# Four nested conditionals for leftover tiles instead of 36, and a plan of 23 places instead of 55

## The chip, the core and the metric

The kernel runs on one core of a Trainium2 chip. The metric is the device time of one execution in microseconds (us); the time given is the median of several executions.

## What is computed

Two blocks follow each other. The first is a gated linear recurrence over 4 batches, 8 heads, 768 steps and head dimension 48; its output, laid out as 3072 rows of 384, is the input of a mixture of 8 experts, of which each row takes two, chosen by noisy logits.

```python
for t in range(S):
    state = alpha[:, :, t, :, None] * state + np.einsum('bhd,bhe->bhde', k[:, :, t], v[:, :, t])
    y[:, :, t] = np.einsum('bhd,bhde->bhe', q[:, :, t], state)
...
noisy_logits = x @ w_gate + np.log1p(np.exp(x @ w_noise)) * noise
top2 = np.argpartition(-noisy_logits, 2, axis=1)[:, :2]
top2_l = top2_l - top2_l.max(-1, keepdims=True)
top2_w = np.exp(top2_l)
top2_w /= top2_w.sum(-1, keepdims=True) + 1e-09
for e in range(E):
    for k in range(2):
        mask = top2[:, k] == e
        h = np.maximum(x[mask] @ w1[e], 0.0)
        out[mask] += top2_w[mask, k, None] * (h @ w2[e])
```

All is float32. With N = 3072 rows and two experts for each there are 6144 row-expert entries, 768 for each expert on average. w1 of an expert is 384 x 1024, w2 is 1024 x 384.

## The kernel before

**Recurrence.** The 3072 steps are worked in NT = 24 chunks of C = 128. The order of the work is written out by hand in the block at the end of the kernel function; the loop over chunks issues loads, transposes, scans, scores, state and output of neighbouring chunks interleaved. Rows of the result go to x_rows in HBM. The routing of a unit of six chunks (`routing`) is a generator; each call of `route` or `route_on` runs its next piece, so that small vector operations are strewn among the others. Entries (row, gate, other expert, rank) are scattered by indirect transfers into `table`, which has a region of 3072 rows for each expert.

**Pairs.** 24 fixed steps follow, `pair_steps`, each for 256 entries of one expert: three for every expert, first one each, then two each. A step has a list of times on a scale where a pair takes T = 20; `work` sorts the steps of all pairs, of the half tiles and of `beside()` by these times, and `until` issues them in that order. A pair gathers its rows by index, multiplies by w1 and w2 on TensorE (PE) with sums formed on VectorE (DVE), scales by the gate on ScalarE (ACT), adds the row of an earlier expert (`get_prev`, `combine`) and scatters the result to the output (`put_pair`). The indirect transfers are issued by GpSimd (POOL), weights by SyncE (SP).

**Leftovers.** 24 pairs hold 768 entries of each expert. What an expert has above that goes to half tiles of 64 entries, of which there are places for NHALF = 3 (`half_tiles`), worked between pairs, and then to whole tiles of 128. Whole tiles stand behind a conditional at the end of the kernel: `more_i` is the number of such tiles plus `again`, a count of rows for which the fast form of the recurrence is not valid. If it is above zero, `last_tiles` works tile after tile, each one nested in the conditional of the tile before, NFULL = 36 deep; then, if `again_i` (the count of rows alone) is above zero, `again_by_levels` does everything anew in a general way, with 24 chunks by levels and 55 tiles.

```python
any_more = nc.values_load(more_i[0:1, 0:1], min_val=0, max_val=NTILE + 3 * C,
...
with tc.If(any_more > 0):
    ...
    redo = nc.values_load(again_i[0:1, 0:1], min_val=0, max_val=3 * C,
    ...
    with tc.If(redo > 0):
```

**Plan.** Where the tiles of variable place begin is computed on DVE in `plan_rest`, once all counts are known (`counted`, `tiles_of`, L774 and L776). `plan` has NTILE = 55 places: 3 half tiles, 16 for the second and third pairs, 36 whole tiles. For each place `given` holds, per expert, how many entries earlier places have taken (55 x 9 values per partition); `first_rows` makes from it the expert (column 0 of plan, L803) and the first row of the table (column 1, L810). The larger operations are L853 and L855 (`gone`), L858 (`given`), L787, L789 and L862 (the share of whole tiles), L794 and L796 in `begun`, and L801, L805, L807, L809 in `first_rows`. `base_of` is a constant of the same shape, set on POOL in `place_slots` (L129 to L142). The pieces are issued by `route_on(3)` in the eighth and the tenth pair. Readers of the plan are `of_plan` (L891), a register load on SP or POOL, ahead of the loads of table rows and weights for half tiles and for the later pairs, and `find_rows` and `choose_rows`, which read `given`.

`out_of_range` (L452 to L457) makes `again` at the sixth pair, and before the change its integer copy `again_i` (L456).

Sequencer instructions of the conditional carry the line L1408, the register load of its count L1406, and what stands at the end of the program L1443.

Of the kernel before, what the change touches and what calls it, by code (L numbers as in the profile page):

```python
# [9 lines left out]
F32 = mybir.dt.float32  # L10
# [3 lines left out]
ALU = mybir.AluOpType  # L14
# [4 lines left out]
def kernel(  # L19
# [32 lines left out]
    nc = tc.nc  # L52
    B, H, S, D = q.shape
    N, DM = out.shape
    E, _, F = moe_w1.shape
    C = 128
# [10 lines left out]
    HC = C // 2  # L67
# [3 lines left out]
    EV = E + 1  # L71
    NTILE = (2 * N) // C + E - 1
# [4 lines left out]
    R2 = 2 * C  # L77
# [2 lines left out]
    AFTER_GROUP = (3, 5, 7)  # L80
    FIRST_PAIR = NHALF
    FIRST_FULL = NHALF + 2 * E
    NFULL = NTILE - FIRST_FULL
    assert R2 * NPAIR == 2 * N and NFULL * C >= 2 * (N - 3 * R2)

    def pool(name, bufs, on=ctx, **kw):
        return on.enter_context(tc.tile_pool(name=name, bufs=bufs, **kw))
# [33 lines left out]
                   allow_small_or_imprecise_dtypes=True)  # L121

    half_no = const.tile([C, NTILE], F32, name="half_no")
    base_of = const.tile([C, NTILE, EV], F32, name="base_of")
    of_slot = const.tile([C, NTILE], F32, name="of_slot")

    def place_slots():
        pairs = base_of[:, FIRST_PAIR:FIRST_FULL].rearrange("p (g b) e -> p g b e", b=2)
        nc.gpsimd.memset(base_of, float(3 * R2))  # L129
        nc.gpsimd.affine_select(out=pairs, in_=pairs, pattern=[[1, E], [0, 2], [1, EV]], compare_op=ALU.is_gt,  # L130
                                fill=float(R2), base=1 - E, channel_multiplier=0)
        nc.gpsimd.affine_select(out=pairs[:, :, 1], in_=pairs[:, :, 1], pattern=[[1, E], [1, EV]],
                                compare_op=ALU.not_equal, fill=float(2 * R2), base=1 - E, channel_multiplier=0)
        nc.gpsimd.iota(of_slot[:, FIRST_PAIR:FIRST_FULL], pattern=[[-1, E], [0, 2]], base=E - 1, channel_multiplier=0,
                       allow_small_or_imprecise_dtypes=True)
        groups = (0,) + AFTER_GROUP + (E,)
        for j in range(NHALF):
            nc.gpsimd.memset(base_of[:, j, 0:E - AFTER_GROUP[j]], float(R2))
            nc.gpsimd.memset(half_no[:, j:j + 1], float(j))
        for j in range(NHALF + 1):  # L140
            nc.gpsimd.memset(half_no[:, FIRST_PAIR + 2 * groups[j]:FIRST_PAIR + 2 * groups[j + 1]], float(j))
        nc.gpsimd.memset(half_no[:, FIRST_FULL:NTILE], float(NHALF))  # L142


    x_rows = dram.tile([N, DM], F32, name="x_rows")
# [133 lines left out]
    def fast_gla(on):  # L279
# [169 lines left out]
        def out_of_range(part):  # L449

            if part:
                out_of = chunks["out_of"]  # L452
                count = few(on, [C, 3], "count", True)
                nc.tensor.matmul(count, ones, out_of[:, 2:5], start=True, stop=True)
                nc.vector.tensor_reduce(out=again, in_=count[0:1, :], axis=mybir.AxisListType.X, op=ALU.add)
                nc.vector.tensor_copy(out=again_i, in_=again)  # L456
                return  # L457
            out_of = chunks["out_of"] = one.tile([C, 5], F32, name="out_of")
            nc.vector.tensor_copy(out=out_of[:, 4:5], in_=short)
            nc.vector.tensor_reduce(out=out_of[:, 0:1], in_=P_end.rearrange("p n j -> p (n j)"),  # L460
                                    axis=mybir.AxisListType.X, op=ALU.min)
            nc.vector.tensor_reduce(out=out_of[:, 1:2], in_=above, axis=mybir.AxisListType.X, op=ALU.max)
            nc.vector.tensor_scalar(out=out_of[:, 2:3], in0=out_of[:, 0:1], scalar1=2 * RANGE, scalar2=None,
                                    op0=ALU.is_lt)
            nc.vector.tensor_scalar(out=out_of[:, 3:4], in0=out_of[:, 1:2], scalar1=0.0, scalar2=None, op0=ALU.is_gt)
# [330 lines left out]
        nc.vector.reduce_sum(out=of, in_=behind, axis=mybir.AxisListType.X)  # L796

    def first_rows(rp, of):
        shape = [C, NTILE, EV]
        behind = rp.tile(shape, F32, name="behind")  # L800
        nc.vector.tensor_tensor(behind, expert_idv[:, None, :].to_broadcast(shape), of[:, :, None].to_broadcast(shape),  # L801
                                op=ALU.is_equal)
        nc.vector.tensor_scalar(out=plan[:, :, 0], in0=of, scalar1=float(E - 1), scalar2=None, op0=ALU.min)  # L803
        at = rp.tile(shape, F32, name="at_row")
        nc.vector.tensor_tensor(at, given, region[:, None, :].to_broadcast(shape), op=ALU.add)  # L805
        yield
        nc.vector.tensor_mul(at, at, behind)  # L807
        first = rp.tile([C, NTILE], F32, name="first")
        nc.vector.reduce_sum(out=first, in_=at, axis=mybir.AxisListType.X)  # L809
        nc.vector.tensor_scalar(out=plan[:, :, 1], in0=first, scalar1=float(TROWS - C), scalar2=None, op0=ALU.min)  # L810

    def plan_all(on):
        rp = on["one"]
# [9 lines left out]
            pass  # L823

    def plan_rest(on):

        rp = on["one"]
        total = counted(on)
# [15 lines left out]
        start, ends = running(rp, ready)  # L844
        nc.vector.tensor_copy(out=tiles_i, in_=ends[0:1, E - 1:E])
        nc.vector.tensor_tensor(more_i, ends[0:1, E - 1:E], again, op=ALU.add)
        yield
        begun(rp, of_slot[:, 0:NHALF], tile_no[:, 0:NHALF], which)
        begun(rp, of_slot[:, FIRST_FULL:NTILE], tile_no[:, 0:NFULL], ends)
        yield  # L850
        shape = [C, NTILE, EV]
        gone = rp.tile(shape, F32, name="at_row")
        nc.vector.tensor_tensor(gone, half_no[:, :, None].to_broadcast(shape), which[:, None, :].to_broadcast(shape),  # L853
                                op=ALU.is_ge)
        nc.vector.tensor_tensor(gone, gone, half[:, None, :].to_broadcast(shape), op=ALU.mult)  # L855
        yield
        fulls = given[:, FIRST_FULL:NTILE]
        nc.vector.scalar_tensor_tensor(given, gone, float(HC), base_of, op0=ALU.mult, op1=ALU.add)  # L858
        yield
        at = rp.tile(shape, F32, name="behind")[:, 0:NFULL]  # L860
        of_expert(at, NFULL, start, ready)
        nc.vector.scalar_tensor_tensor(fulls, at, float(C), fulls, op0=ALU.mult, op1=ALU.add)  # L862
        yield
        yield from first_rows(rp, of_slot)


    WHY = "computed from the counts, in range by construction"
# [94 lines left out]


    def last_tiles(i, whole_tile):
        if i == NFULL:
            return
        number = nc.values_load(tiles_i[0:1, 0:1], min_val=0, max_val=NTILE,
                                skip_runtime_bounds_check_because="a count of tiles")
        with tc.If(number > i):
            whole_tile(FIRST_FULL + i)  # L970
            last_tiles(i + 1, whole_tile)
# [436 lines left out]
    with tc.If(any_more > 0):  # L1408
        with ExitStack() as es:
            order.update(puts=[], gets=[])  # L1410
            last_tiles(0, whole_tiles(pools(es, "l_")))
        redo = nc.values_load(again_i[0:1, 0:1], min_val=0, max_val=3 * C,
                              skip_runtime_bounds_check_because="a count of at most 3 C rows")
        with tc.If(redo > 0):
            taken.clear()
            order.update(puts=[], gets=[])
            again_by_levels()
# [30 lines left out]
```

## Time and profile before

| what | value |
|---|---|
| median of 3 runs | 691.13 us (690.56 to 694.62) |
| the profiled execution | 710.9 us, its span 709.2 us |
| PE busy | 675.1 us (95% of the span) |
| DVE busy | 455.0 us (64%) |
| POOL busy | 300.4 us (42%) |
| ACT busy | 260.3 us (37%) |
| mean granted TensorE clock | 0.983 |
| last matmul ends | 692.0 us |
| last scatter to the output is issued | 693.4 us |

The span runs from the first to the last instruction of the profiled execution. Busy times are those of the engines; register loads, branches, semaphore waits and the issuing of transfers are sequencer instructions and not counted as busy. In lists, L853 is line 853 of the kernel, "xcount" the number of instructions, the number after the bar the busy time in us and the mean ns of one. In a timeline the columns are start and length in us, engine, line, operation, output <- inputs, shapes, and in brackets how long the engine had been idle and what released it. A line of a wait table reads: who waited, for whom, us in total, times, longest.

### The profile page before, as it was taken

What the parts mean: (1) busy time and instruction counts of PE and PEld (TensorE: products, weight loads), DVE (VectorE), ACT (ScalarE), POOL (GpSimd) and SP (SyncE); (2) the same over time, 40 slices, a digit from 0 to 9 for tenths busy, and PEclk for the clock granted to TensorE, in tenths of its full rate; (3) what the DMA queues carried; (4) which work ended last, traced back from release to release, by engine and by line L of the source; (5) the groups of instructions that cost most, each with busy time, mean ns of one, the idle gap of its engine ahead of it and who ended that gap; (6) DMA issues with size and microseconds to landing.
All of it is one profiled execution on the core that took longest, in us unless ns stands there. A gap on an engine that the chain in (4) does not pass through costs nothing.

```text
span 709.2 us, 15155 instructions
## 1 busy us (share of the span) xinstructions
PE 675.1 (95%) x5777; PEld 628.9 (89%) x5777; DVE 455.0 (64%) x1058; ACT 260.3 (37%) x561; POOL 300.4 (42%) x390
## 2 busy tenths in 40 slices
PE   7999999999999997999999999999999999999990
PEld 5888877878999997989999999988999889999890
DVE  8777867856778774877466667464565646645440
ACT  4456545444443323222333332333332233323330
POOL 5442483764234573586322335412453224533121
PEclk9999999999999998999999999999999999999996
DMA  9777576567866754575413457137351574521110
GB/s 177 169 154 156 129 135 136 127 129 212 285 201 221 224 150 129 198 198 189 141 37 123 136 193 261 54 130 271 117 199 60 174 251 135 157 60 38 32 45 24
DMA packets 145861, 105.64 MB, mean 149 GB/s; under 512 B 110931, under 2 KB 133151, under 8 KB 145780
## 3 DMA queue, kind: packets, MB, share of 16 engines
q1 hardware_dynamic: 134132, 80.41, 40.8%
q0 software_dynamic: 11504, 23.76, 10.8%
q8 instruction: 48, 0.79, 0.5%
q10 hardware_dynamic: 144, 0.41, 0.2%
q14 instruction: 33, 0.27, 0.1%
HBM read 95.19 MB, written 14.96 MB: 155 GB/s over the span
## 4 chain that ended last, share of the span: by engine, by line
PE 53%; issue 6%; POOL 1%; another core or an unknown queue 1%; ACT 1%; DMA 1%; DVE 0%; POOLq 0%; ACTq 0%; DVEq 0%
PE sc L1127 22%; PE o_ps L1134 13%; PE h_ps L1134 10%; PE h_ps L1127 4%; PE x_ps L1065 2%; PE half_ps L1297 1%; PE h_half_ps L1283 1%; DMA out_dram<-prev,where 1%; POOL out_dram L879 0%; POOL prev L871 0%; POOL x_in L886 0%; ACT L651 0%; ACT m L1205 0%; ACT m L1203 0%
## 5 line engine op out<-in xcount | busy, mean ns | idle before, releaser
L886 POOL DMA_INDIRECT x_in<-x_rows,where x48 | 52.6, 1095 | 138.0 <-PE h_ps L1134 87.8
L871 POOL DMA_INDIRECT prev<-out_dram,where x48 | 54.1, 1127 | 67.4 <-issue 29.6
L1127 PE MATMUL sc<-xs,ws 128*128 128x128 f32 x576 | 74.5, 279 | 2.2 <-ACT m L1205 1.9
L879 POOL DMA_INDIRECT out_dram<-prev,where x48 | 51.7, 1076 | 58.7 <-DVE prev L1155 43.3
L1127 PE MATMUL sc<-xt,w 128*128 128x128 f32 x576 | 73.9, 279 | 0.0
L1127 PEld LDWEIGHTS sc<-xs,ws 128*128 128x128 f32 x576 | 69.1, 194 | 3.1 <-ACT m L1205 2.5
L1134 PE MATMUL o_ps<-wt,hx 128*128 128x192 f32 x384 | 70.6, 327 | 0.2 <-issue 0.2
L1127 PEld LDWEIGHTS sc<-xt,w 128*128 128x128 f32 x576 | 70.8, 196 | 0.0
L1138 ACT ACTIVATE h<-h 128x512 f32<-128x512 f32 x72 | 45.4, 631 | 64.1 <-DVE h L1074 60.9
L1074 DVE TENSOR_TENSOR h<-sc,m 128x512 f32<-128x512 f32 x48 | 33.1, 692 | 50.0 <-PE sc L1127 45.1
L1134 PEld LDWEIGHTS o_ps<-wt,hx 128*128 128x128 f32 x384 | 63.5, 190 | 0.9 <-issue 0.5
L161 POOL DMA_INDIRECT table<-entry,place_u x48 | 53.0, 1105 | 15.9 <-issue 14.6
L1127 PE MATMUL sc<-xs,w 128*128 128x128 f32 x384 | 49.3, 282 | 1.2 <-DVE h L1074 1.2
L1127 PEld LDWEIGHTS sc<-xs,w 128*128 128x128 f32 x384 | 44.9, 192 | 4.8 <-DVE h L1074 3.8
L369 POOL TENSOR_TENSOR k_P<-k_P,over 128x512 f32<-128x512 f32 (+1 forms) x25 | 28.8, 1153 | 47.8 <-DVE over L353 36.5
L1127 PE MATMUL h_ps<-xt,w 128*128 128x128 f32 x384 | 47.1, 276 | 0.0
L326 PE MATMUL tp<-ident,ins 128*128 128x128 f32 x288 | 42.9, 285 | 4.0 <-issue 2.9
L1127 PEld LDWEIGHTS h_ps<-xt,w 128*128 128x128 f32 x384 | 44.8, 192 | 0.2
L1143 ACT ACTIVATE o<-o_ps,tab 128x192 f32<-128x192 f32 x23 | 9.6, 419 | 96.0 <-PE o_ps L1134 86.1
L345 DVE TENSOR_TENSOR_SCAN P_all<-shared,least 128x516 f32<-128x516 f32 (+1 forms) x25 | 30.3, 1216 | 17.8 <-ACT shared L340 9.5
L1074 DVE TENSOR_TENSOR h<-h_ps,m 128x512 f32<-128x512 f32 x24 | 16.6, 691 | 36.9 <-PE h_ps L1127 33.5
L326 PEld LDWEIGHTS tp<-ident,ins 128*128 128x128 f32 x288 | 31.4, 143 | 9.2 <-issue 4.0
(235 smaller groups left out, 1411.9 us busy)
## 6 DMA issues: line engine op xcount, KB each, us to landing
w<-in_moe_w_dram SPq DMA_DIRECT2D x30, 1536.0 KB
ins<-in_alpha_dram SPq DMA_DIRECT2D x24, 192.0 KB
ins<-in_k_dram SPq DMA_DIRECT2D x24, 192.0 KB
ins<-in_q_dram SPq DMA_DIRECT2D x24, 192.0 KB
vt<-in_v_dram SPq DMA_DIRECT2D x24, 192.0 KB
x_rows<-y_sb SPq DMA_DIRECT2D x24, 192.0 KB
ins<-in_moe_w_dram SPq DMA_DIRECT2D x3, 1536.0 KB
shared<-in_moe_w_dram SPq DMA_DIRECT2D x3, 1536.0 KB
```

The costliest lines, as they stand in the source:

```text
L161: put = nc.gpsimd.indirect_dma_start(out=table, out_offset=bass.IndirectOffsetOnAxis(ap=place, axis=0), in_=entry, in_offset=None, bounds_ ...
L326: nc.tensor.transpose(tp[:, j, :], src[:, 2 * j:2 * j + 2, :], ident)
L345: nc.vector.tensor_tensor_scan(P_all[:, at], a_all[:, at], least.rearrange("p j t -> p (j t)")[:, at], 0.0, op0=ALU.mult, op1=ALU.max)
L369: nc.gpsimd.tensor_tensor(c["k"][:, at], c["k"][:, at], over[:, at, 1:CB], op=ALU.mult)
L871: get = nc.gpsimd.indirect_dma_start(out=rows.bitcast(U32), out_offset=None, in_=out.bitcast(U32), in_offset=bass.IndirectOffsetOnAxis(ap= ...
L879: put = nc.gpsimd.indirect_dma_start(out=out, out_offset=bass.IndirectOffsetOnAxis(ap=at, axis=0), in_=rows, in_offset=None, bounds_check= ...
L886: nc.gpsimd.indirect_dma_start(out=rows, out_offset=None, in_=x_rows[0:units * UT, :], in_offset=bass.IndirectOffsetOnAxis(ap=at, axis=0), ...
L1065: nc.tensor.transpose(x_ps[:, a, :], x_in[i % 2][:, s, ds(a * C, C)], ident)
L1074: nc.vector.tensor_tensor(to, p, q, op=ALU.add)
L1127: nc.tensor.matmul(bank[name][:, f, :], W[:, ds(f * C, C)], X, start=new and f == 0, stop=True, skip_group_check=True)
L1134: nc.tensor.matmul(bank[name], H[:, f, :], W[:, f, :], start=new and f == 0, stop=True, skip_group_check=True)
L1138: nc.scalar.activation(t, t if src is None else src, AF.Relu)
```

## The change

The plan gets NPLAN = 19 + NLAST = 23 places instead of 55, with NLAST = 4 for whole tiles. All operations of `plan_rest` and `first_rows` work on the first 23 places of the same tiles; `plan_all`, which belongs to the general way, still works on 55. `last_tiles` nests four tiles instead of 36. A new count `over`, the number of whole tiles above four, is added to `again` to make `again_i`, so that with more than four whole tiles left the general way computes everything anew; the copy in `out_of_range` goes. `base_of` has 23 places.

```diff
@@ -80,8 +80,9 @@
     AFTER_GROUP = (3, 5, 7)
     FIRST_PAIR = NHALF
     FIRST_FULL = NHALF + 2 * E
-    NFULL = NTILE - FIRST_FULL
-    assert R2 * NPAIR == 2 * N and NFULL * C >= 2 * (N - 3 * R2)
+    NLAST = 4
+    NPLAN = FIRST_FULL + NLAST
+    assert R2 * NPAIR == 2 * N
 
     def pool(name, bufs, on=ctx, **kw):
         return on.enter_context(tc.tile_pool(name=name, bufs=bufs, **kw))
@@ -121,7 +122,7 @@
                    allow_small_or_imprecise_dtypes=True)
 
     half_no = const.tile([C, NTILE], F32, name="half_no")
-    base_of = const.tile([C, NTILE, EV], F32, name="base_of")
+    base_of = const.tile([C, NPLAN, EV], F32, name="base_of")
     of_slot = const.tile([C, NTILE], F32, name="of_slot")
 
     def place_slots():
@@ -139,7 +140,7 @@
             nc.gpsimd.memset(half_no[:, j:j + 1], float(j))
         for j in range(NHALF + 1):
             nc.gpsimd.memset(half_no[:, FIRST_PAIR + 2 * groups[j]:FIRST_PAIR + 2 * groups[j + 1]], float(j))
-        nc.gpsimd.memset(half_no[:, FIRST_FULL:NTILE], float(NHALF))
+        nc.gpsimd.memset(half_no[:, FIRST_FULL:NPLAN], float(NHALF))
 
 
     x_rows = dram.tile([N, DM], F32, name="x_rows")
@@ -453,7 +454,6 @@
                 count = few(on, [C, 3], "count", True)
                 nc.tensor.matmul(count, ones, out_of[:, 2:5], start=True, stop=True)
                 nc.vector.tensor_reduce(out=again, in_=count[0:1, :], axis=mybir.AxisListType.X, op=ALU.add)
-                nc.vector.tensor_copy(out=again_i, in_=again)
                 return
             out_of = chunks["out_of"] = one.tile([C, 5], F32, name="out_of")
             nc.vector.tensor_copy(out=out_of[:, 4:5], in_=short)
@@ -796,18 +796,19 @@
         nc.vector.reduce_sum(out=of, in_=behind, axis=mybir.AxisListType.X)
 
     def first_rows(rp, of):
-        shape = [C, NTILE, EV]
-        behind = rp.tile(shape, F32, name="behind")
+        K = of.shape[1]
+        shape = [C, K, EV]
+        behind = rp.tile([C, NTILE, EV], F32, name="behind")[:, 0:K]
         nc.vector.tensor_tensor(behind, expert_idv[:, None, :].to_broadcast(shape), of[:, :, None].to_broadcast(shape),
                                 op=ALU.is_equal)
-        nc.vector.tensor_scalar(out=plan[:, :, 0], in0=of, scalar1=float(E - 1), scalar2=None, op0=ALU.min)
-        at = rp.tile(shape, F32, name="at_row")
-        nc.vector.tensor_tensor(at, given, region[:, None, :].to_broadcast(shape), op=ALU.add)
+        nc.vector.tensor_scalar(out=plan[:, 0:K, 0], in0=of, scalar1=float(E - 1), scalar2=None, op0=ALU.min)
+        at = rp.tile([C, NTILE, EV], F32, name="at_row")[:, 0:K]
+        nc.vector.tensor_tensor(at, given[:, 0:K], region[:, None, :].to_broadcast(shape), op=ALU.add)
         yield
         nc.vector.tensor_mul(at, at, behind)
-        first = rp.tile([C, NTILE], F32, name="first")
+        first = rp.tile([C, NTILE], F32, name="first")[:, 0:K]
         nc.vector.reduce_sum(out=first, in_=at, axis=mybir.AxisListType.X)
-        nc.vector.tensor_scalar(out=plan[:, :, 1], in0=first, scalar1=float(TROWS - C), scalar2=None, op0=ALU.min)
+        nc.vector.tensor_scalar(out=plan[:, 0:K, 1], in0=first, scalar1=float(TROWS - C), scalar2=None, op0=ALU.min)
 
     def plan_all(on):
         rp = on["one"]
@@ -823,6 +824,7 @@
             pass
 
     def plan_rest(on):
+
 
         rp = on["one"]
         total = counted(on)
@@ -844,24 +846,28 @@
         start, ends = running(rp, ready)
         nc.vector.tensor_copy(out=tiles_i, in_=ends[0:1, E - 1:E])
         nc.vector.tensor_tensor(more_i, ends[0:1, E - 1:E], again, op=ALU.add)
+        over = rp.tile([1, 1], F32, name="over")
+        nc.vector.tensor_scalar(out=over, in0=ends[0:1, E - 1:E], scalar1=-float(NLAST), scalar2=0.0, op0=ALU.add,
+                                op1=ALU.max)
+        nc.vector.tensor_tensor(again_i, over, again, op=ALU.add)
         yield
         begun(rp, of_slot[:, 0:NHALF], tile_no[:, 0:NHALF], which)
-        begun(rp, of_slot[:, FIRST_FULL:NTILE], tile_no[:, 0:NFULL], ends)
+        begun(rp, of_slot[:, FIRST_FULL:NPLAN], tile_no[:, 0:NLAST], ends)
         yield
-        shape = [C, NTILE, EV]
-        gone = rp.tile(shape, F32, name="at_row")
-        nc.vector.tensor_tensor(gone, half_no[:, :, None].to_broadcast(shape), which[:, None, :].to_broadcast(shape),
+        shape = [C, NPLAN, EV]
+        gone = rp.tile([C, NTILE, EV], F32, name="at_row")[:, 0:NPLAN]
+        nc.vector.tensor_tensor(gone, half_no[:, 0:NPLAN, None].to_broadcast(shape), which[:, None, :].to_broadcast(shape),
                                 op=ALU.is_ge)
         nc.vector.tensor_tensor(gone, gone, half[:, None, :].to_broadcast(shape), op=ALU.mult)
         yield
-        fulls = given[:, FIRST_FULL:NTILE]
-        nc.vector.scalar_tensor_tensor(given, gone, float(HC), base_of, op0=ALU.mult, op1=ALU.add)
+        fulls = given[:, FIRST_FULL:NPLAN]
+        nc.vector.scalar_tensor_tensor(given[:, 0:NPLAN], gone, float(HC), base_of, op0=ALU.mult, op1=ALU.add)
         yield
-        at = rp.tile(shape, F32, name="behind")[:, 0:NFULL]
-        of_expert(at, NFULL, start, ready)
+        at = rp.tile([C, NTILE, EV], F32, name="behind")[:, 0:NLAST]
+        of_expert(at, NLAST, start, ready)
         nc.vector.scalar_tensor_tensor(fulls, at, float(C), fulls, op0=ALU.mult, op1=ALU.add)
         yield
-        yield from first_rows(rp, of_slot)
+        yield from first_rows(rp, of_slot[:, 0:NPLAN])
 
 
     WHY = "computed from the counts, in range by construction"
@@ -962,7 +968,7 @@
 
 
     def last_tiles(i, whole_tile):
-        if i == NFULL:
+        if i == NLAST:
             return
         number = nc.values_load(tiles_i[0:1, 0:1], min_val=0, max_val=NTILE,
                                 skip_runtime_bounds_check_because="a count of tiles")
@@ -1409,8 +1415,8 @@
         with ExitStack() as es:
             order.update(puts=[], gets=[])
             last_tiles(0, whole_tiles(pools(es, "l_")))
-        redo = nc.values_load(again_i[0:1, 0:1], min_val=0, max_val=3 * C,
-                              skip_runtime_bounds_check_because="a count of at most 3 C rows")
+        redo = nc.values_load(again_i[0:1, 0:1], min_val=0, max_val=NTILE + 3 * C,
+                              skip_runtime_bounds_check_because="a count of tiles and rows")
         with tc.If(redo > 0):
             taken.clear()
             order.update(puts=[], gets=[])
```

## The prediction

> **What bounds the kernel now.** I first asked in which stages the tensor engine stops, because the change takes work from the vector engine and from code that is jumped over. The table by stage splits the span into the recurrence (to 240 us), the overlap with the first expert pairs (to 320), the pairs alone (to 692), and the end.
>
> ```profile
> core 0: us, PE busy (x) PEld busy (x) DVE busy (x) ACT busy (x) POOL busy (x), PEclk, DMA share, GB/s
> 240.00:320.00 80.00, 72.90 (x528) 70.76 (x527) 55.00 (x139) 25.34 (x49) 50.57 (x57) 0.96 0.62 180
> 320.00:692.00 372.00, 371.85 (x2740) 355.57 (x2739) 216.80 (x537) 122.40 (x242) 133.09 (x125) 1.00 0.41 133
> 692.00:709.20 17.20, 0.01 (x1) 0.00 (x0) 0.80 (x3) 0.00 (x0) 2.02 (x2) 0.59 0.07 24
> ```
>
> In the third row PE is busy 371.85 of 372.00 us. The waits of PE in that same stretch are this one line:
>
> ```profile
> PE sc L1127 <- ACT m L1205: 0.2, 1, 0.2
> ```
>
> So from 320 us on nobody holds PE back, and a shorter job elsewhere can give back at most 0.2 us. Next I looked for where the plan is computed. The timeline of DVE shows it spread over two pairs, 357 to 374 us and 397 to 414 us, all inside that stretch. Its first part, as far as it matters here:
>
> ```profile
> 370.22 0.13 DVE L845 CAST tiles_i<-ends 1x1 int32<-1x1 f32 x1
> 370.28 0.14 DVE L846 TENSOR_TENSOR more_i<-ends,again 1x1 int32<-1x1 f32 x1
> 370.35 0.40 DVE L1146 SCALAR_TENSOR_TENSOR o<-h_ps,tab,n 128x192 f32<-128x192 f32 x1
> 371.04 0.42 DVE L1146 SCALAR_TENSOR_TENSOR o<-o_ps,tab,n 128x192 f32<-128x192 f32 x1 [0.30 <-PE o_ps L1134]
> ```
>
> The bracket says that DVE itself had 0.30 us to spare before the second summing. Last I looked at what the skipped code costs at the end, by the instructions of the conditional's line:
>
> ```profile
> L1408 POOLq EVENT_SEMAPHORE  x6: 17/30/604, 696.3 to 697.3; - x6
> L1408 SPq COMPARE_BRANCH  x1: 50/50/50, 605.7 to 605.7; - x1
> L1408 PEldq COMPARE_BRANCH  x1: 3457/3457/3457, 690.5 to 690.5; - x1
> L1408 POOLq COMPARE_BRANCH  x1: 53/53/53, 693.3 to 693.3; - x1
> L1408 POOLq INC_SWDGE_SEM  x1: 2287/2287/2287, 697.4 to 697.4; - x1
> ```
>
> Each engine branches once, over everything; no line of a leftover tile ran. The 36 nested conditionals are thus never entered: not one of them costs an executed instruction. What is paid is one jump per engine and the catching up of semaphores behind it.
>
> [...] after the branch POOL's next record comes at 696.32, 2.95 us later, SP's at 611.46, 5.67 us later, and PE's branch lasts 3.46 us. [...]
>
> **The change part by part.**
>
> *Plan of 23 places.* Seven operations go from 55 x 9 = 495 to 23 x 9 = 207 elements. They take 0.664 (L853), 0.676 (L855), 0.665 (L858), 0.665 (L801), 0.667 (L805), 0.661 (L807) and 0.670 us (L809), together 4.67. [...] a line through this trace's 0.665 at 495 and 0.357 at 192 elements (L774) gives 0.372. New: 7 x 0.372 = 2.60, saved 2.06 us. Five operations go from 324 to 36 elements: L794 0.495, L796 0.491, L787 0.487, L789 0.495, L862 0.497, together 2.47; a 27-element one takes 0.177 (L794, first form), so 36 is put at 0.187, five make 0.94, saved 1.53. Two plan writes (L803 0.197, L810 0.205) go from 55 to 23 elements, about 0.03 each, 0.07. Sum: 3.66 us less on DVE.
>
> *The new count.* One tensor_scalar and one tensor_tensor of a single element come in behind L846, one cast (L456, 0.141 at 333.3) goes. Nearest rows: L845 0.134 and L846 0.139, so +0.14 of busy time; the second reads the first, and dependent operations of this chain start 0.2 us apart (L839 at 369.10, L841 at 369.30), so the queue is held 0.27 us. Behind them stands the summing L1146 at 370.35. It moves to about 370.6 and ends near 371.0; the next L1146 starts at 371.04 because PE hands it over then, with 0.30 idle ahead of it. So 0.27 goes into that idle time; PE rewrites the same bank at 372.14, another 0.68 us after the read ends at 371.46. If both covers were gone it would cost 0.27 us, once. Net on DVE: -3.5 us of 455.0.
>
> *What hides it.* PE has no wait in either stretch, so -3.5 us of DVE gives 0 us of time, with ends 0 and -0.2 (the one PE wait of the whole stage). The plan itself is ready about 0.9 us sooner: from L787 on three operations save 0.31 each, but the summing L1146 at 412.47 waits for PE (its product ends near 412.1 in the record), and only the 0.3 each of L807 and L809 and little more are left behind it. The waiter is SP's queue (21.2 us at L891, ended by L810 at 414.4), with the half tile's table rows and weights behind it. They are first used by DVE at 436.8 (L905) and by PE at 464.0 (L1283): 22 us of cover, so arriving 0.9 sooner starts the transfers sooner and ends nothing sooner. DMA was busy 0.38 of the stretch 394 to 414 and 0.80 of that after, and PE stood in neither.
>
> *POOL's setting up.* The memset of base_of (L129) goes from 495 to 207 elements, 0.519 us against some 0.26 (256 elements take 0.302, 128 take 0.195); that of half_no at L142 from 36 to 4, about 0.03. POOL gets to S (L420, 42.30) up to 0.3 us sooner; its next product k_P waits 2.86 us for DVE anyhow. Taken as -0.1, ends 0 and -0.3.
>
> *32 conditionals fewer.* None was executed. The jump still goes over four tiles, the whole general way (24 chunks and 55 tiles)[...]: 0 saved. The record does not show whether the catching up depends on how much is skipped, so I bound it. POOL's skipped indirect transfers fall from 36 x 3 + 48 + 55 x 3 = 321 to 4 x 3 + 48 + 165 = 225, to 0.70. If INC_SWDGE_SEM (2.29) and the 8.65 us drain of POOL after it scaled with that, 0.30 x 10.94 = 3.3 us would go; if they do not, 0. I take 0: the instruction is executed once, whatever sum it adds. From the other side, [...] SP's 5.67 instead of 2.95 would cost 2.7 - 0.6 = 2.1[...].
>
> Sum against the profiled execution (710.9 us, span 709.2): 0 + 0 - 0.1 = 710.8. That execution stands 19.8 us above the median of the runs shown, 691.13; taken off: 691.0 us.
>
> **The rivals.**
> - *The tail scales with what is skipped* (faster): 691.1 - 3.3 = 687.8 us. For it: 17.2 us pass after the last matmul, most in POOL's records. Against it: one execution of one instruction.
> - *DVE is the bound in these two pairs* (faster): 691.1 - 3.5 = 687.6. For it: DVE runs without a gap from 366.3 to 371. Against: PE never waits there.
> - *The jump's target is dearer* (slower): place, the end of POOL's queue; price up to 3.1 us, 694.2[...]. For it: the spread 2.95 to 5.67 among engines. Against: [...] SP's runs 100 us before the end, beside other traffic.
> - *The change does something else: the general way is taken.* 55 tiles load 3 MB of weights each, 169 MB, at the page's mean 149 GB/s some 1130 us more: over 1800 us. Excluded as good as: it lies inside the outer conditional, whose count more_i is not changed and was zero.
>
> **How the numbers follow.** Within 1% is about what a measurement of this kernel can tell from no change, 6.9 us. No change to the path: 0.78. Tail scales: 0.06. DVE: 0.04. Dearer target: 0.08. General way: 0.01. Something not seen (placement of buffers in memory moved by 1,152 bytes): 0.03, halved. All but the fourth rival lie within 1% at their own centres; past it I put 0.01 of each faster one and half of the unseen (0.035), and 0.03 of the dearer target, the general way and the other half (0.055). Same: 0.91. The shown runs spread from 690.56 to 694.62, so the range is 687.5, where the faster rivals stand, to 694.5, where the slower one stands.
>
> **What would show it.** In the profile after: the plan's operations at 0.37 and 0.19 us, DVE's total near 451.5; PE still busy over 99.9% between 320 us and its last matmul; SP's wait for the plan about 0.9 us shorter with nothing behind it sooner on PE; one COMPARE_BRANCH per engine at the end; INC_SWDGE_SEM again near 2.3 us and POOL's drain again near 8.7. It is wrong if the drain or INC_SWDGE_SEM follows the skipped transfers, if the records between POOL's branch and its first semaphore grow past 3.6 us, or if PE shows a new wait near 371 or 412 us.

## The result: 0.46 per cent slower, and the profile after

The kernel after takes 697.1 us (median of 20 runs, 692.3 to 700.4), the kernel before on the same chip 693.6 us (20 runs, 690.6 to 697.2): ratio 1.0046, interval 1.0026 to 1.0066. It is a small slowdown, but a real one; the forecast was no change. Ratios compare runs within 1.5 per cent of the fastest of their kernel; on the chip of e1 to e4, where the kernel before spreads from 710.8 to 730.4 us, that rule keeps 32 of its 75 runs but all 22 of e4, so the medians of all runs are compared there instead.

The profiled execution of before (710.9 us) was an outlier, 17 us above the median of its kernel, with TensorE idle for 3.2 and 1.7 us at 270 to 273 us; the two spans, 709.2 and 695.6, can't be set against each other. What can be compared is each stretch on its own.

The table by stage of the kernel after (columns as before), with the end of the last matmul at 677.8 us:

```profile
core 0: us, PE busy (x) PEld busy (x) DVE busy (x) ACT busy (x) POOL busy (x), PEclk, DMA share, GB/s
240.00:320.00 80.00, 79.69 (x601) 78.81 (x600) 63.38 (x161) 29.32 (x57) 56.40 (x59) 1.00 0.65 191
320.00:677.80 357.80, 357.49 (x2644) 341.73 (x2642) 202.70 (x513) 118.05 (x233) 125.59 (x118) 1.00 0.40 134
677.80:695.60 17.80, 0.00 (x0) 0.00 (x0) 0.80 (x3) 0.00 (x0) 2.02 (x2) 0.58 0.07 23
```

In the pairs PE is busy 357.49 of 357.80 us, and its only wait there is again one of a fraction of a microsecond:

```profile
PE sc L1133 <- DVE h L1080: 0.3, 1, 0.3
```

The plan's operations in the timeline of DVE (start, duration):

```profile
355.83 0.14 DVE L848 TENSOR_TENSOR more_i<-ends,again 1x1 int32<-1x1 f32 x1
355.89 0.13 DVE L850 TENSOR_SCALAR over<-ends 1x1 f32<-1x1 f32 x1
356.06 0.15 DVE L852 TENSOR_TENSOR again_i<-over,again 1x1 int32<-1x1 f32 x1
...
357.37 0.20 DVE L794 TENSOR_TENSOR behind<-tile_no,ends 128x36 f32<-128x36 f32 x1
...
358.24 0.36 DVE L859 TENSOR_TENSOR at_row<-half_no,which 128x207 f32<-128x207 f32 x1
```

They are as small as worked out (0.36 and 0.20 us), and DVE's total is 451.8 us. The instructions of the conditional's line, the last two of which are POOL's:

```profile
L1414 POOLq EVENT_SEMAPHORE  x6: 17/30/1591, 681.7 to 683.7; - x6
...
L1414 SPq COMPARE_BRANCH  x1: 50/50/50, 591.5 to 591.5; - x1
...
L1414 PEldq COMPARE_BRANCH  x1: 3757/3757/3757, 676.3 to 676.3; - x1
...
L1414 POOLq COMPARE_BRANCH  x1: 53/53/53, 679.1 to 679.1; - x1
L1414 POOLq INC_SWDGE_SEM  x1: 2287/2287/2287, 683.8 to 683.8; - x1
```

INC_SWDGE_SEM takes 2.287 us as before, and from the last matmul to the end it is 17.8 us against 17.2. This tail ranges from 17.1 to 18.2 us in the traces of all runs below, with the conditionals of before (17.1 to 18.2) and of after (17.1 to 18.0) alike. So none of the places that the diff names has become slower by 3 us. The time was lost where the diff has no line: in the first 16 us. The timeline of PE there, first of the kernel before (start, duration, operation, number, and in brackets PE's idle time ahead of it with what ended it):

```profile
1.33 2.50 PE L1357 MATMUL y<-ones 128*128 128x128 f32 x6 [1.33 <-POOL ones L99]
3.78 2.52 PE L326 MATMUL tp<-ident,ins 128*128 128x128 f32 x12
6.54 0.63 PE L326 MATMUL tp<-ident,ins 128*128 128x128 f32 x4 [0.23 <-DMA ins<-in_alpha_dram]
7.00 0.93 PE L1357 MATMUL y<-ones 128*128 128x128 f32 x4
8.61 1.41 PE L390 MATMUL sc<-q_P,k_P 48*128 48x128 f32 x16 [0.67 <-POOL k_P L369]
9.94 0.66 PE L326 MATMUL tp<-ident,ins 128*128 128x128 f32 x4
```

and of the kernel after:

```profile
1.33 2.50 PE L1363 MATMUL y<-ones 128*128 128x128 f32 x6 [1.33 <-POOL ones L100]
4.32 4.68 PE L327 MATMUL tp<-ident,ins 128*128 128x128 f32 x16 [0.48 <-DMA ins<-in_alpha_dram]
8.79 1.48 PE L1363 MATMUL y<-ones 128*128 128x128 f32 x4
10.20 2.08 PE L391 MATMUL sc<-q_P,k_P 48*128 48x128 f32 x16
12.21 1.11 PE L327 MATMUL tp<-ident,ins 128*128 128x128 f32 x4
```

Two things are to be seen. After, PE stops for 0.48 us for the first load, and the sixteen transposes of the first four loads end at 9.0 instead of 7.2 us. And four transposes take 1.11 us at 12.2 where they take 0.66 before: TensorE still runs at half speed, the transposes starting 213 ns apart instead of 109. The trace's first record of the full clock is at 14.9 us, before at 5.7. Matmul 75 starts 2.2 us later than before, and this lag stays 2.2 us to matmul 1000 (at 88 us). (Matmul 200 below means the 200th matmul that the trace has; its lag is how much later than in the kernel before it starts.) The two stretches in the table by stage, before:

```profile
0.00:16.00 16.00, 12.47 (x98) 9.47 (x98) 13.01 (x23) 6.02 (x13) 8.43 (x36) 1.00 0.91 176
16.00:160.00 144.00, 138.86 (x1713) 117.36 (x1711) 107.16 (x205) 74.05 (x186) 76.86 (x136) 0.99 0.69 142
```

and after:

```profile
0.00:16.00 16.00, 13.68 (x73) 10.33 (x74) 11.45 (x21) 5.37 (x11) 6.83 (x31) 1.00 1.25 149
16.00:160.00 144.00, 143.35 (x1808) 122.73 (x1807) 113.53 (x214) 77.52 (x195) 84.75 (x143) 1.00 0.87 145
```

In the first 16 us PE does 73 matmuls instead of 98, and the DMA share (second number from the end) is 1.25 instead of 0.91 while fewer bytes move (149 instead of 176 GB/s): the same packets take longer. (The PEclk column reads 1.00 there in both, since it has no record ahead of the first one; durations decide.) The list of queues puts it on one of them, before and after:

```profile
q1 hardware_dynamic: 134132, 80.41, 40.8%
```

```profile
q1 hardware_dynamic: 134132, 80.41, 45.7%
```

The packet records of q1 show which: the 98,304 packets of 192 bytes (the rows of a, k, q and v) take 16.2 ns in the mean before and 20.5 after; those of 1536 and 4096 bytes hardly change (75 and 195 ns before, 78 and 190 after). The mean over the run hides how uneven this is: of the packets that start in the first 16 us it is 15.7 ns before and 25.5 after, and yet the first load's 1,024 packets take 16.2 ns in both, the second load's 19.8, and from the third on they take 25 to 28.

The signals by which the first four loads report that they have landed, one after the other, come at 3.64, 4.52, 5.54 and 6.40 us before and at 4.18, 5.38, 6.60 and 7.77 us after.

**Where that comes from.** A row of 48 numbers is 192 bytes, and rows of a, k and q lie 256 bytes apart in `ins`. base_of shrinks from 55 x 9 to 23 x 9 numbers, 1,152 bytes for each partition, and everything behind it in SBUF moves down by that: 4 x 256 + 128. In the built programs ins begins at byte 40,992 before, 32 behind a multiple of 256, so that a row fills bytes 32 to 224 of one block; after, it begins at 39,840, 160 behind one, and every row reaches 96 bytes over the next boundary. That the boundary is what costs is shown by the runs below: in the mean of the run a packet of 192 bytes takes 16.0 to 16.3 ns where the rows of a, k and q stay inside a block and 20.5 to 21.0 where all of them reach into the next, 4.3 ns more in the kernel after than before. How the hardware comes to this price is not shown.

### The profile page after: what moved, and what is told of

It is laid out like the page before. It is cut to its first block, busy times and chain, and to the rows that moved or that the text cites. A ratio compares the mean times of both kernels' runs of the same rounds, so it can differ in the third digit from the quotient of the medians.

```text
span 695.6 us, 15157 instructions
## 1 busy us (share of the span) xinstructions
PE 672.3 (97%) x5777; PEld 629.4 (90%) x5777; DVE 451.8 (65%) x1059; ACT 260.1 (37%) x561; POOL 305.4 (44%) x390
## 4 chain that ended last, share of the span: by engine, by line
PE 54%; issue 6%; POOL 1%; DMA 1%; ACT 0%; DVE 0%; POOLq 0%; DVEq 0%
PE sc L1133 22%; PE o_ps L1140 14%; PE h_ps L1140 10%; PE h_ps L1133 5%; PE x_ps L1071 2%; PE half_ps L1303 1%; PE h_half_ps L1289 1%; DMA out_dram<-prev,where 1%; POOL out_dram L885 0%; POOL prev L877 0%; POOL x_in L892 0%; ACT L651 0%; PE x_ps L1282 0%; POOL prev_half L877 0%; DVE wt L1077 0%
## 5 line engine op out<-in xcount | busy, mean ns | idle before, releaser
L885 POOL DMA_INDIRECT out_dram<-prev,where x48 | 53.3, 1110 | 57.2 <-DVE prev L1161 41.8
L1133 PE MATMUL sc<-xs,ws 128*128 128x128 f32 x576 | 73.1, 276 | 0.3 <-ACT m L1204 0.3
L1133 PE MATMUL sc<-xt,w 128*128 128x128 f32 x576 | 72.2, 275 | 0.0
L1133 PEld LDWEIGHTS sc<-xt,w 128*128 128x128 f32 x576 | 69.1, 192 | 0.0
L162 POOL DMA_INDIRECT table<-entry,place_u x48 | 54.8, 1141 | 16.0 <-issue 14.7
L370 POOL TENSOR_TENSOR k_P<-k_P,over 128x512 f32<-128x512 f32 (+1 forms) x25 | 28.8, 1152 | 39.5 <-DVE over L354 28.4
L327 PE MATMUL tp<-ident,ins 128*128 128x128 f32 x288 | 45.0, 293 | 0.8 <-DMA ins<-in_alpha_dram 0.5
L1080 DVE TENSOR_TENSOR h<-h_ps,m 128x512 f32<-128x512 f32 x24 | 16.6, 690 | 36.4 <-PE h_ps L1133 36.4
```

Of the source, the lines that this page charges most:

```text
L162: put = nc.gpsimd.indirect_dma_start(out=table, out_offset=bass.IndirectOffsetOnAxis(ap=place, axis=0), in_=entry, in_offset=None, bounds_ ...
L327: nc.tensor.transpose(tp[:, j, :], src[:, 2 * j:2 * j + 2, :], ident)
L370: nc.gpsimd.tensor_tensor(c["k"][:, at], c["k"][:, at], over[:, at, 1:CB], op=ALU.mult)
L885: put = nc.gpsimd.indirect_dma_start(out=out, out_offset=bass.IndirectOffsetOnAxis(ap=at, axis=0), in_=rows, in_offset=None, bounds_check= ...
L1080: nc.vector.tensor_tensor(to, p, q, op=ALU.add)
L1133: nc.tensor.matmul(bank[name][:, f, :], W[:, ds(f * C, C)], X, start=new and f == 0, stop=True, skip_group_check=True)
```

## The experiments

Theories: *placement* (the crossing rows cost the time), against *the change itself* (plan, count or jump). Within placement: *start* (only the first loads are on the path) against *everywhere*; and, from e5 on, *clock* (the late loads delay TensorE's full clock) against *load* (their lateness itself).

The runs e1 to e4 were made on a chip on which the kernel before takes 721.9 us, e5 to e8 on a second (693.4) and e9 to e12 on a third (693.5). Ratios are to the kernel before on the same chip. The time in ns is the mean of all packets of 192 bytes in the run, v's rows among them.

**e1: the kernel before, unchanged.**

> The kernel before, unchanged. Every theory: ratio 1.000. It gives an ordinary profiled execution of the kernel before (the one shown was 19.8 us above its median): placement theory expects its 192-byte packets near 16 ns, as in the first one (16.2), against 20.5 in the kernel after.

721.72 us against 721.87, ratio of the medians 0.9998 (0.9990 to 1.0014), 16.0 ns, full clock at 6.0 us. With 22 runs on this chip a ratio is known to some 0.2 per cent, about half of the loss that is looked for; so the traces have to carry the argument.

**e2: the kernel after, with base_of's old size.**

```diff
-    base_of = const.tile([C, NPLAN, EV], F32, name="base_of")
+    base_of = const.tile([C, NTILE, EV], F32, name="base_of")[:, 0:NPLAN]
```

> The kernel after, with base_of allocated at 55 places and used at 23, so that every buffer behind it lies where it lay before; all else of the change is in. Placement theory (rows of 192 bytes that a load writes into ins begin at byte 160 of 256 in the kernel after and cross into the next 256; here they begin at byte 32 as before): ratio 1.000, packets of 192 bytes 16 ns. Jump theory (the slower end) and plan theory (new count or shorter operations on the path): ratio 1.0046 as in the kernel after, packets no matter.

721.76 us, ratio of the medians 0.9999 (0.9982 to 1.0022), 16.1 ns, matmul 200 at +0.16 us. All of the change is in it but the move of the buffers, and nothing of the loss is to be seen.

**e3 and e4: the kernel before, moved by 32 and by 128 bytes.**

```diff
-    base_of = const.tile([C, NTILE, EV], F32, name="base_of")
+    base_of = const.tile([C, NTILE * EV + 8], F32, name="base_of")[:, 0:NTILE * EV]
+    base_of = base_of.rearrange("p (n e) -> p n e", e=EV)
```

(+ 32 instead of + 8 in e4.)

> The kernel before, base_of 32 bytes longer, so that ins begins at byte 64 of 256 and a row of 192 bytes just fits in. Placement theory: ratio 1.000, 192-byte packets 16 ns. If any shift of the buffers costs time: ratio 1.003 to 1.006. Jump and plan theories: 1.000.

722.13 us, ratio of the medians 1.0004 (0.9989 to 1.0034), 16.1 ns: rows end on the boundary, and nothing happens.

> The kernel before, base_of 128 bytes longer, so that ins begins at byte 160 of 256 as in the kernel after; nothing else of the change. Placement theory: ratio 1.0046 (1.003 to 1.006), 192-byte packets 20.5 ns. Jump and plan theories: 1.000.

722.99 us, ratio of the medians 1.0016 (0.9997 to 1.0033), 20.6 ns, full clock at 15.6 us, matmul 200 at +2.36 us. None of the change is in it but the move, and the whole lag of the kernel after is in its trace; the time is longer too, but by itself it would not settle the matter. With e2 and, below, e11, which have the change without the crossing and no lag, the change itself is out.

**e5: moved by 64 bytes** (+ 16 in the same edit).

> The kernel before with base_of's buffer 64 bytes longer, so that ins begins at byte 96 of a 256-byte block and every row of 192 bytes reaches over the next boundary by its last 32 bytes only. Crossing theory [...]: mean packet of 192 bytes 20 to 21 ns, matmuls 2 to 2.5 us later from 16 us on, ratio 1.003 to 1.007. Size-of-the-spill theory (the cost grows with the bytes beyond the boundary, 96 in the kernel after): a third of the difference, mean packet 17 to 18 ns, 0.8 us, ratio 1.001 to 1.002. No-placement theory (the shift by 128 bytes was slow for another reason): 16 ns and 1.000.

695.07 us, 1.0028 (1.001 to 1.0047). The packets answer as the crossing theory says, with the whole price for 32 bytes beyond the boundary as for 96: 21.0 ns (20.6 in e4), not a third of the difference. The lag does not: matmul 75 comes only 0.43 us late and matmul 225 0.7, though the packets of the first four loads end at 6.42 us as in e4 (6.45; 5.84 before) and their signals come at 4.08, 5.28, 6.47 and 7.65 us (e4: 4.08, 5.28, 6.50 and 7.66). What differs is the full clock, at 9.2 instead of 15.6 us. PE in e5, then in e4:

```profile
4.21 4.66 PE L327 MATMUL tp<-ident,ins 128*128 128x128 f32 x16 [0.38 <-DMA ins<-in_alpha_dram]
...
10.87 0.66 PE L327 MATMUL tp<-ident,ins 128*128 128x128 f32 x4
```

```profile
4.21 4.68 PE L327 MATMUL tp<-ident,ins 128*128 128x128 f32 x16 [0.38 <-DMA ins<-in_alpha_dram]
...
12.11 1.11 PE L327 MATMUL tp<-ident,ins 128*128 128x128 f32 x4
```

The sixteen transposes are the same in both; the next four take 0.66 and 1.11 us. So the lag has a second link, which the theory lacked: loads that land at the same times cost 0.4 to 0.7 us with the early full clock and 2.4 us with the late one, in one trace each. (The two are from two chips; e7 below, on e5's chip, is like e4: 14.9 us and +2.22.)

**e6 to e8: which loads count.** The first three chunks' a, k and q go to nine tiles of the pair stage that are still unused:

```diff
+        def place_of(x, n):
+            return on["early"][3 * n + "akq".index(x)] if n < NIN else ins[x][n % NIN]
...
-            a_t = transposed(ins["a"][n % NIN])
+            a_t = transposed(place_of("a", n))
...
+        on["early"] = [t.rearrange("p f t -> p (f t)").rearrange("p (h d) -> p h d", h=H)
+                       for t in (hs[0] + hs[1] + hx + m)[0:3 * NIN]]
```

(k and q likewise; the memsets of ins and of the state move behind those of these tiles.) In e7 less_1, which lies between ins and these tiles, gets 128 bytes more; in e8 base_of and less_1 do.

> The kernel before, but the first three chunks' a, k and q land in nine tiles that the pair stage uses later (h00 to h11, hx, m), which begin at byte 64 of a 256-byte block: rows [64, 256) fit; later chunks use ins as before, whose rows fit too. Reference for the next two. Both theories: mean packet 16 ns, ratio 0.997 to 1.002 (the fourth chunk's loads needn't wait for the first chunk's buffers, which may help a little).

> As e6, but the nine tiles begin at byte 192 of a block, so the rows of the first three chunks cross a boundary and those of all later chunks fit. Start theory (only the loads before 16 us are on the path): slower than e6 by 1.2 to 2.5 us, ratio to the kernel before 1.002 to 1.006, mean packet over the whole run close to 16.6 ns (9 of 72 loads cross). Everywhere theory (the added DMA time costs throughout the 24 chunks): under 0.4 us over e6, ratio like that of e6.

> As e6, but ins begins at byte 160 of a block: the rows of the first three chunks fit and those of all later chunks cross. Start theory: within 0.5 us of e6, although the mean packet is near 20 ns. Everywhere theory: nearly the whole 3 to 5 us of the shifted kernel, ratio 1.004 to 1.006.

Measured: e6 692.84 us, 1.0009 (0.9983 to 1.0036), 16.3 ns; e7 695.73 us, 1.0026 (1.0008 to 1.0044), 17.4 ns (16.6 expected); e8 691.90 us, 0.9985 (0.9965 to 1.0004), 19.7 ns. The table by stage, e6, then e7, then e8:

```profile
0.00:16.00 16.00, 13.32 (x97) 10.49 (x98) 12.96 (x22) 5.96 (x12) 9.65 (x44) 1.00 0.95 188
16.00:160.00 144.00, 143.38 (x1808) 122.86 (x1808) 114.10 (x220) 78.08 (x197) 85.09 (x141) 1.00 0.70 143
```

```profile
0.00:16.00 16.00, 13.66 (x73) 10.31 (x74) 11.43 (x21) 5.38 (x11) 8.15 (x40) 1.00 1.24 153
16.00:160.00 144.00, 143.37 (x1808) 122.73 (x1808) 113.31 (x213) 77.54 (x195) 85.00 (x143) 1.00 0.70 145
```

```profile
0.00:16.00 16.00, 12.76 (x96) 9.98 (x97) 12.91 (x24) 5.96 (x12) 9.70 (x42) 1.00 0.99 180
16.00:160.00 144.00, 143.38 (x1808) 122.76 (x1808) 113.63 (x218) 78.16 (x197) 85.46 (x143) 1.00 0.86 144
```

With the first loads crossing, the first row is like that of the kernel after (73 matmuls, share 1.24) and the second that of before; with the later ones crossing it is the other way round. Against e6, the matmuls of e7 are 2.12 us late from the 200th on and stay so to the 2000th (166 us); those of e8 are 0.02 to 0.04 us late over the same stretch, although the DMA share between 16 and 160 us is 0.86 instead of 0.70. Of e7 less e8, 3.8 us by medians, a part is chance; the start theory needs 2.1. "Everywhere" is out.

**e9 to e12: clock or load.** `warm(3)` at the start, three products of ones that keep PE busy, becomes `warm(5)`: in the kernel after (e9) and in the kernel before (e10).

> The kernel after with five warming products in front of the first transposes instead of three, so that TensorE is busy until 5.5 us and runs behind the late loads without a gap (in the kernel after it stops at 3.83 us for 0.48 us, and three more times for 0.1 us). The rows still cross: mean packet of 192 bytes near 20.5 ns. Clock theory (the late loads break TensorE's first busy stretch, and the full clock then comes at 15 us instead of 6 to 8.5; the half-speed work between is most of the loss): full clock before 9.5 us, matmul 200 at most 0.9 us behind the kernel before, ratio 0.999 to 1.002. Load theory (the late loads themselves carry the loss): the lag stays 2.2 us or grows by the two products, ratio 1.004 to 1.006.

> The same five warming products in the kernel before: the control for e9. Clock theory: the full clock comes at 6 us as it does anyway and the two products push the first transposes back by up to 1.6 us of work at half speed, of which the loads hide a part: ratio 0.999 to 1.002. If it falls below 0.998, the kernel before loses time to a late clock in many executions too, and what e9 gains is not only the loss of the crossing.

> The kernel after, unchanged, on the chip of e9 to e11, for a direct comparison with them: ratio 1.003 to 1.006, mean packet 20.5 ns. Clock theory: full clock at about 15 us; load theory: no matter when.

Measured: e12 696.39 us, 1.0032 (1.0013 to 1.005), 20.7 ns, full clock at 15.2 us, matmul 200 at +2.21 us; e9 694.94 us, 1.0016 (0.9997 to 1.0034), 20.6 ns, full clock at 7.3 us; e10 694.24 us, 1.0017 (0.9998 to 1.0036), 16.3 ns, full clock at 9.8 us. The timeline of PE in e9:

```profile
1.33 4.21 PE L1363 MATMUL y<-ones 128*128 128x128 f32 x10 [1.33 <-POOL ones L100]
5.33 3.25 PE L327 MATMUL tp<-ident,ins 128*128 128x128 f32 x16
8.42 0.93 PE L1363 MATMUL y<-ones 128*128 128x128 f32 x4
10.13 1.41 PE L391 MATMUL sc<-q_P,k_P 48*128 48x128 f32 x16 [0.79 <-POOL k_P L370]
11.48 0.65 PE L327 MATMUL tp<-ident,ins 128*128 128x128 f32 x4
```

PE no longer waits for a load, and four transposes take 0.65 us at 11.5. The two products are four more matmuls in the trace, so matmul 204 does here what matmul 200 does elsewhere: it starts at +1.54 us, 0.67 us sooner than in e12 (+2.21), with packets as dear as ever. That is less than the clock theory said, which had allowed a lag of 0.9, and not what the load theory said, which had 2.2 or more. In e10, whose rows fit, the same matmul is at +1.53. That these two agree is partly luck: e10's full clock came later than was expected of it, and e9, with the earlier one, then waits 0.79 us for k_P, a product that hangs on the late loads. By medians the crossing costs 2.9 us without the two products (e12 less e11, below; resampled interval 1.3 to 4.6) and 0.7 us with them (e9 less e10; -0.6 to 1.4). So the two products take away most of what the crossing costs. This alone does not say how: a start of the transposes at 5.33 us also gives the late loads more time to land. That the clock carries most of it is read from e5 beside e4; what the late loads cost by themselves is between nothing and about 1.4 us.

**e11: the kernel after, ins on a boundary, and v's rows 64 numbers apart.**

```diff
-    base_of = const.tile([C, NPLAN, EV], F32, name="base_of")
+    base_of = const.tile([C, NPLAN * EV + 24], F32, name="base_of")[:, 0:NPLAN * EV]
+    base_of = base_of.rearrange("p (n e) -> p n e", e=EV)
...
-        vt = vp.tile([C, H, D], F32, name="vt")
+        vt = vp.tile([C, H, DP], F32, name="vt")[:, :, 0:D]
```

> The kernel after with base_of's buffer 96 bytes longer, so that ins begins on a 256-byte boundary, and with vt's rows of 48 numbers laid 64 apart, so that v's rows fit into one block too (in both kernels three quarters of them cross). Placement theory: mean packet 15 to 15.7 ns, starts as in the kernel before, ratio 0.997 to 1.000, the best of all. If the change itself cost time (plan, new count or the conditionals): 1.003 to 1.006 with packets of 15 ns.

693.50 us, 1.0007 (0.9986 to 1.0028), full clock at 7.5 us, matmul 200 at +0.04. It is faster than the kernel after beside it (696.39) and equal to the kernel before. The second edit brought nothing: the mean packet is 16.3 ns, not 15 to 15.7. So v's rows, which lie without gaps and cross in three of four cases, gain nothing when they fit: in the kernel before, its first two loads take 15.8 and 15.5 ns a packet though they cross. The first crossing load of the kernel after is not dearer either (16.2 ns). Why neither is dearer no run shows.

All fourteen traces in one table (end of the packets of the first four loads; first full clock; matmul 200, in e9 and e10 matmul 204, against matmul 200 of the kernel before, us):

```text
             rows at start  4 loads  clock  lag        rows at start  4 loads  clock  lag
before       fit            5.84     5.7    0     e5   cross          6.42     9.2    0.44
e1           fit            5.73     6.0    0.08  e4   cross          6.45    15.6    2.36
e2           fit            6.00     7.7    0.16  after cross         6.55    14.9    2.20
e3           fit            5.76     8.4    0.06  e7   cross          6.53    14.9    2.22
e6           fit            5.76     8.5    0.11  e12  cross          6.46    15.2    2.21
e8           fit            5.82     7.0    0.13  e9   cross, warm 5  6.47     7.3    1.54
e11          fit            5.79     7.5    0.04  e10  fit, warm 5    5.81     9.8    1.53
```

**The times at equal granted clock.** Each run has its mean granted clock on record, and much of the spread between runs of one kernel goes with it: a straight line through the runs of a chip falls by 0.80 to 0.96 us for each 0.001. (The half-speed work ahead of the first clock record does not enter this mean.) Fitted with one slope for each chip (a single run of 971 us left out), the difference to the kernel before at equal clock, with a resampled 95% interval, in us:

```text
e1   fit    -0.2 (-0.9 to 0.5)     e5   cross          1.8 (1.2 to 2.4)
e2   fit     0.5 (-0.4 to 1.4)     e4   cross          1.7 (0.8 to 2.5)
e3   fit     0.1 (-0.6 to 0.8)     e7   cross          1.7 (1.2 to 2.3)
e6   fit    -0.3 (-0.9 to 0.2)     e12  cross          2.3 (1.6 to 2.9)
e8   fit    -1.2 (-1.7 to -0.7)    e9   cross, warm 5  1.8 (1.2 to 2.4)
e11  fit     0.1 (-0.6 to 0.8)     e10  fit, warm 5    1.3 (0.8 to 1.8)
```

Leaving out the two with five products, the kernels whose first rows cross lie at 1.7 to 2.3 us and those whose first rows fit at -1.2 to 0.5; the traces have 2.2 to 2.4 us (e5: 0.4) and at most 0.2 us at matmul 200. e5 stands with the others, so that trace is probably not its usual case. e7 less e6 is 2.0 us (1.4 to 2.7), e12 less e11 2.2 (1.3 to 3.1), e9 less e10 0.5 (-0.2 to 1.1). Why e8 comes out below the kernel before is not known; up to matmul 2000 its trace does not differ from that of e6.

## Why the prediction was wrong

**Right, step by step.** The plan's operations were put at 0.372 and 0.187 us and took 0.36 and 0.19 to 0.20; DVE's total was put at 451.5 and is 451.8. The new count goes into DVE's slack, no new wait of PE appears near it. SP's wait for the plan fell from 21.2 to 20.3 us, the 0.9 forecast, and nothing came sooner for it. The 32 conditionals give nothing: one branch for each engine, INC_SWDGE_SEM at 2.287 us and POOL's drain at 8.65 us, all three untouched by the smaller number of skipped transfers. POOL's first semaphore comes 2.6 us after its branch (2.95 before). That answers the rivals: the tail doesn't scale, DVE is not the bound, the target isn't dearer where it would count (PE's branch lasts 0.30 us longer, but POOL ends the kernel), the general way isn't taken. The 3.1 us for a dearer target were the author's estimate from the trace of before: SP's 5.67 us less POOL's 2.95, less the 0.6 us of POOL's longest semaphore record, and 1.0 us for a stop that SP makes among its semaphores; what the engines wait for behind the branch was not shown. The forecast's sums come out, but for one without weight: 55 tiles with two pieces of weights of 1,536 KB each load 173 MB, not 169 (the 149 GB/s there are the DMA's mean in the profile before).

**Wrong: the term that was never priced.** "Something not seen (placement of buffers in memory moved by 1,152 bytes): 0.03, halved" stood in the chances and not in the sum. The step on POOL's setting up took base_of's smaller size for what it saves, 0.1 us, and not for what lies behind it. That rows would cross could have been worked out: 1,152 is 128 off a multiple of 256, and rows of 192 bytes at 256-byte pitch leave 64 bytes to spare, so with a move by 128 they cross at the old place, at the new one or at both; the built program says which. That a crossing costs time had to be measured. The start had its signs as well: in the first 16 us the kernel before has a DMA share of 0.91, and PE runs right behind its loads (at 6.54 us it waits 0.23 us for one). The forecast looked for what bounds the kernel only from 240 us on, where the changed lines run; the row of its table for the first 240 us was left out.

**The chain that took its place.** Rows cross; the first four loads report 1.20 us apart instead of 0.92 (4.18 to 7.77 and 3.64 to 6.40). Four transposes at half speed (213 ns apart) take 0.9 us (from 12.21 to 13.12, where the next work starts, in the kernel after), so PE, which ran behind the loads with gaps of at most 0.1 us until its clock had risen, now stops four times (0.48, 0.11, 0.14 and 0.08 us); the full clock comes mostly at about 15 us instead of 5.7 to 8.5; what PE does in between takes up to twice as long (transposes start 213 ns apart instead of 109). The first links, from the crossing to the late loads and the lag, are shown by e2, e4, e7 and e8. That the gaps put off the full clock is read from the traces: it came late in four of five traces with these gaps and in none of nine without. With gaps of at most 0.1 us the full clock comes at 5.7 to 9.8 us, 4.4 to 8.5 us after the first matmul at 1.33, and hardly twice at the same time. With the longer gaps four of five traces have it at 14.9 to 15.6 us and one, e5, at 9.2. Nearly the same gaps can thus cost 0.4 or 2.4 us; how often they cost the one or the other is not known from one trace for each kernel, and what sets the time of the full clock is not shown.

**Sizes.** The trace has 2.2 us at matmul 200; the median of after lies 3.5 us above before (interval of the ratio: 1.8 to 4.6 us), that of e12 2.9 us, and 2.3 us at equal clock. The rest is probably chance in the granted clock of the later stages: it is 0.9877 in the mean of the 20 runs of after, 0.9886 in those of e12 and 0.9889 in the runs of before beside e12, and 0.001 goes with 0.8 us there, so that about 1 us of the 3.5 would be that (an estimate; the clock of the 20 runs of before is not on record). No link from the crossing to it shows: e4, e5 and e7 have the mean clock of the kernel before within about 0.0001. Of the 6.1 us between forecast and measurement the other 2.6 is the base: 691.13 was a median of three, and 20 runs of the same kernel give 693.61.

## What to carry to other kernels

A buffer that changes its size moves the buffers allocated behind it: base_of, 1,152 bytes smaller, moved ins by 1,152. Take the move modulo 256 (128 here, and packets of 192 bytes went from 16.2 to 20.5 ns) and look up which DMA targets with short rows lie behind it, before any operation is priced. Look also at the first microseconds: where TensorE ran right behind its loads at half speed, loads that came 1.20 instead of 0.92 us apart went with a full clock at 14.9 to 15.6 us in four of five traces, against 5.7 to 8.5 in the seven traces with the same start whose first rows fit. Two more dummy products ahead of the transposes made this start nearly insensitive to the crossing (0.5 us, -0.2 to 1.1), but cost 1.3 us themselves (e10, at equal clock), so the better remedy here is to place the rows so that they fit (e11).

## What was not expected of the hardware

- In kernels whose rows of 192 bytes reach into a second 256-byte block of SBUF, packets of this size take 20.5 to 21.0 ns instead of 16.0 to 16.3 in the mean of the run, and 25 to 26 instead of 15.4 to 15.7 in the first 16 us, where such loads follow each other. The mean is about the same for 32 bytes beyond the boundary (e5, 21.0) as for 96 (e4, 20.6). The first such load is no dearer than one that fits (16.2 ns), nor are the first two of v in the kernel before (15.8 and 15.5).
- Under these loads this shows only where the transfers are waited for: in e8 the dearer packets run for over 120 us beside PE (DMA share 0.86 instead of 0.70 between 16 and 160 us) and delay it by 0.04 us at most; in e7, where only the first rows cross, it is 2.12 us.
- The same kernel takes 693 us on two chips (mean granted clock 0.989) and 722 us on another (0.976).
